# Borders from attention to feed-forward in a new order, two residual adds moved to TensorE, weight pieces stored a tile later

## The chip, the core and the metric

The program runs on one core of one Trainium2 chip. The metric is the device time of one execution in microseconds. TensorE is PE, its weight loads PEld, VectorE DVE, ScalarE ACT, GpSimd POOL; SP (SyncE) issues all DMAs.

## What is computed

Four layers over x of 2048 x 512 (bf16), attention, feed-forward, attention, feed-forward, and then all gradients of that chain for a given grad_out. The two layers, with layernorm LN without scale or shift:

```python
def A(h, wqkv, wo):                       # 32 heads of 16
    q, k, v = split(h @ wqkv)
    pq, pk = phi(q), phi(k)               # phi(t) = where(t > 0, t + 1, exp(t)) + 1e-6
    kv = einsum("bhsd,bhse->bhde", pk, v); z = einsum("bhsd->bhd", pk)
    o = einsum("bhqd,bhde->bhqe", pq, kv) / (einsum("bhqd,bhd->bhq", pq, z)[..., None] + 1e-6)
    return o @ wo
def B(h, w_gate, w_up, w_down):
    return (sigmoid(h @ w_gate) * (h @ w_up)) @ w_down
x = x + A(LN(x)); x = x + B(LN(x)); x = x + A(LN(x)); x = x + B(LN(x))
```

Outputs: the last x and the gradients of x, wqkv, wo, w_gate, w_up and w_down.

## The kernel before

The sequence is cut into 16 tiles of 128 rows (`st`), D = 512 into 4 chunks, F = 1376 into three slices of 512, 512 and 352 columns. Layers 0 and 2 are attention, 1 and 3 feed-forward; the backward part follows. In the forward part PE, ACT, DVE and POOL run in the order in which the code writes their instructions (`manual_schedule`), each engine waiting at the head of its own queue; SP's order is left to the tile scheduler. A DMA issue also waits for the one eight before it.

`kq_fwd` is the attention layer. A loop over tiles makes phi(k) (`pk_all`), phi(q) (`pq_all`, but for the last two tiles) and accumulates X = h^T pk in four PSUM banks. After the loop comes the border: z (sum of pk, broadcast by matmuls with ones), X to SBUF (`X_sb`), kv = Wv^T X masked by head (`kvbdT`), M = kv Wo (`M_sb`), the last two q projections (`late_q`), and MT for the backward part. With M, attention of a tile is one product.

`attn_fronts` has a tile's steps: `prod` (pq times z, POOL or DVE), `front1` (DVE reduces to `den`), `front2` (DVE adds eps, takes the reciprocal `rden_all`, multiplies to `pqnstage`), `front3` (PE transposes it, an engine copies to `pqnT`), `attn_mm` (PE, four matmuls into `y_ps`), `attn_add` (DVE adds the residual into `xs[st]`, then `ln_stats`: bn_stats and bn_aggr on DVE, three small POOL operations). `FwdLN.apply` normalizes on ACT (`hstage`), `stage_T` transposes on PE and copies to `hT`. `attn_y` is `attn_mm` and `attn_add`.

`ab_fwd` is the feed-forward loop. In tile `st` it runs `gu` for three slices (8 matmuls into `g_ps` and `u_ps`, two sigmoids on ACT, `hh_t` on DVE, one multiply into `ssd_t` on POOL), transposes hh into `hhT`, and `finish` of the tile before: 11 matmuls into `y_ps`, the add into `xs` on DVE and, in layer 1 alone, the next layer's `ln_stats`. Between them stand the attention steps of tiles ahead: `FLAG` = 3 for prod and fronts, `YLAG` = 2 for the output. `ssd_t` and `hh_t` have two buffers, so tile st + 2 waits for the stores of tile st. In layer 1 each tile from 1 on also runs one of 13 units of `wT_units`: a transposing load of a weight piece into one of two buffers (`wt_st`), and its store to DRAM for the backward part.

PSUM: `t`, `g`, `u` two banks each, `y` and `ln` one each. All transposes of fronts and `stage_T` share `ln`; attention outputs and `finish` share `y`.

Of the kernel before, what the change touches and what calls it, by code (L numbers as in the profile page):

```python
# [60 lines left out]
def kernel(  # L61
# [78 lines left out]
    with tc.tile_pool(name="wfwd", bufs=1, reuse_waits="tile") as wfwd, ExitStack() as lctx, tc.manual_schedule(engines=EM):  # L140
# [44 lines left out]
        with tc.tile_pool(name="aq0", bufs=1, reuse_waits="tile") as aq:  # L185
            A = kq_fwd(k, aq, 0, lns[0], lns[1], x_bf)
            with tc.tile_pool(name="wt_stage", bufs=2, reuse_waits="tile") as wt_stage:
                units = wT_units(k, wt_stage, A_wqkv, A_wo, B_w_gate, B_w_up, B_w_down)
                A.tail()
                ab_fwd(k, A, lns[1], {st + 1: u for st, u in enumerate(units)}, nxt=lns[2])  # L190
        xctx.close()
        with tc.tile_pool(name="aq2", bufs=1, reuse_waits="tile") as aq:
# [45 lines left out]
            A.tail()  # L238
# [140 lines left out]
def wT_units(k, stage, A_wqkv, A_wo, B_w_gate, B_w_up, B_w_down):  # L379
    nc = k.nc  # L380
    units = []

    def by_rows(src, c0, n, dst):
        def unit():
            t = stage.tile([P, NDC, D], BF16, name="wt_st")
            nfull = min(n, F // P - c0) if src.shape[-1] == F else n
            nc.sync.dma_start(out=t[:, 0:nfull, :], in_=src[:, c0 * P:(c0 + nfull) * P], transpose=True)
            if nfull < n:
                nc.sync.dma_start(out=t[:, nfull, :], in_=src[:, F - P:F], transpose=True)
            nc.sync.dma_start(out=dst[c0 * P:(c0 + nfull) * P, :].rearrange("(n p) d -> p n d", p=P),  # L390
                              in_=t[:, 0:nfull, :])
            if nfull < n:
                nc.sync.dma_start(out=dst[(c0 + nfull) * P:F, :], in_=t[P - FLAST:P, nfull, :])
        return unit

    def by_cols(src, f0, w, dst):
        def unit():
            t = stage.tile([P, NDC, D], BF16, name="wt_st")
            v = t[:].rearrange("p a b -> p (a b)")[:, 0:NDC * w].rearrange("p (a b) -> p a b", a=NDC)
            nc.sync.dma_start(out=v, in_=src[f0:f0 + w, :], transpose=True)  # L400
            nc.sync.dma_start(out=dst.rearrange("(c p) f -> p c f", p=P)[:, :, f0:f0 + w], in_=v)
        return unit

    for f0, w in FSL:
        units.append(by_cols(B_w_down, f0, w, k.wT["wdT"]))
    for src, nm in ((B_w_up, "wuT"), (B_w_gate, "wgT")):
        for c0, n in ((0, 4), (4, 4), (8, 3)):
            units.append(by_rows(src, c0, n, k.wT[nm]))
    for src, nm, C in ((A_wo, "woT", D), (A_wqkv, "wqkvT", 3 * D)):
        for c0 in range(0, C // P, NDC):  # L410
            units.append(by_rows(src, c0, NDC, k.wT[nm]))
    return units
# [20 lines left out]
class FwdLN:  # L433
# [9 lines left out]
    def stats(self, st):  # L443
        if st < NST:
            self.nmr[st] = ln_stats(self.k, self.k.xs[st][:], self.rstd(st))
# [13 lines left out]
    def stage_T(self, st):  # L459
        if st >= NST:  # L460
            return
        k = self.k
        h_t = self.hs.pop(st)
        hT = k.lnres["hT"].tile([P, NDC, P], BF16, name="hT")
        transpose_blocks(k, k.ps["ln"], hT[:], [h_t[:, c * P:(c + 1) * P] for c in range(NDC)], "vector", tag="ln_tp")
        self.hTs[st] = hT
# [60 lines left out]
def kq_fwd(k, aq, l, ln, ln_next, x_src=None):  # L527
# [10 lines left out]
    with ExitStack() as ctx:  # L538
# [4 lines left out]
        if l == 0:  # L543
            MT_sb = big.tile([P, NDC, D], BF16, name="MT_sb")
            X_sb = big.tile([P, NDC, D], BF16, name="X_sb")
        else:
            X_sb = big.tile([P, NDC, D], BF16, name="X_sb")
            MT_sb = big.tile([P, NDC, D], BF16, name="MT_sb")
        cnt = [0]
# [76 lines left out]
        def late_q(st):  # L626
            ps = proj(st, 0, ps_tile(k, "t", [P, D], F32, "t_mm"))
            e_t, a_t = qa_tiles()
            exp_to(e_t, ps)

            def phi():
                clamp(a_t, e_t)
                phi_out(A.pq_all[:, st, :], ps, a_t)
                save_phq(st, a_t)
            return phi
# [69 lines left out]
        z_ps = mm_tile()  # L705
        nc.tensor.matmul(z_ps[:], lhsT=k.ones32[:], rhs=zs, start=True, stop=False)

        def z_mm(st):
            nc.tensor.matmul(z_ps[:], lhsT=k.ones_sq[:], rhs=pk_all[:, st, :], start=False, stop=(st == NST - 1))

        for st in range(NST - ZLAG, NST - 1):
            z_mm(st)
        X_some(NST, NST - 2)
        z_mm(NST - 1)
# [3 lines left out]
        A.front2(0)  # L718
        for ic in range(NDC):
            X_mm(NST - 1, ic)  # L720
            nc.scalar.copy(X_sb[:, ic, :], X_ps[ic][:])
        nc.sync.dma_start(out=sv["X"].rearrange("(c p) j -> p c j", p=P), in_=X_sb[:])

        kv_ps = ps_tile(k, "y", [P, D], F32, "kv_ps")
        kv3 = kv_ps[:].rearrange("p (c f) -> p c f", c=NDC)
        for c in range(NDC):
            cs = slice(c * P, (c + 1) * P)
            for ic in range(NDC):
                nc.tensor.matmul(kv3[:, c, :], lhsT=k.wqkv[:, ic, 2 * D + c * P:2 * D + (c + 1) * P],
                                 rhs=X_sb[:, ic, cs], start=(ic == 0), stop=(ic == NDC - 1))  # L730
        nc.vector.tensor_tensor(kvbdT[:], kv3, k.bdmask[:].unsqueeze(1).to_broadcast([P, NDC, P]), ALU.mult)
        A.front3(0)
        A.prod(1, nc.vector)
        for c in range(NDC):
            m_ps = ps_tile(k, "gu"[c % 2], [P, D], F32, "M_ps")
            nc.tensor.matmul(m_ps[:], lhsT=kvbdT[:, c, :], rhs=k.wo[:, c, :], start=True, stop=True)
            evac_copy(k, A.M_sb[:, c, :], m_ps[:], "vector" if c % 2 else "scalar")
        A.front1(1)
        A.attn_y(0)
        A.front2(1)  # L740
        phis = [late_q(st) for st in range(NST - QLATE, NST)]
        nc.scalar.activation(k.tab[:], k.neg[:], ACT.Sigmoid)
# [6 lines left out]
        A.front3(1)  # L749
        phis[0]()  # L750
        A.ln.apply(0)
        for jc in range(NDC):
            nc.scalar.copy(MT_sb[:, jc, :], mt_ps[jc][:])
        nc.sync.dma_start(out=sv["MT"].rearrange("(c p) j -> p c j", p=P), in_=MT_sb[:])
        A.attn_mm(1)
        phis[1]()
    k.kv[l] = dict(kvbdT=kvbdT, zb=A.zb, rden_all=A.rden_all)

    def tail():
        A.ln.stage_T(0)  # L760
        A.prod(2)
        A.prod(3)
        A.attn_add(1)
        A.front1(2)
        A.front2(2)
    A.tail = tail
# [7 lines left out]
def attn_fronts(k, A, pool, small):  # L774
# [17 lines left out]
    def front2(st):  # L792
# [5 lines left out]
        den = f["den"]  # L798
        f["pqn"] = cur["pqn"][:, st % 2, :]
        nc.vector.tensor_scalar(den[:], den[:], EPS, None, ALU.add)  # L800
        nc.vector.reciprocal(A.rden_all[:, st, :], den[:])
# [6 lines left out]
    def front3(st):  # L808
        if st >= NST:
            return  # L810
        f = F_[st]
        pqnT = pool.tile([P, NDC, P], BF16, name="pqnT", bufs=3)
        transpose_blocks(k, k.ps["ln"], pqnT[:], [f["pqn"][:, c * P:(c + 1) * P] for c in range(NDC)],
                         "scalar", tag="ln_tp")
        f["T"] = pqnT

    def attn_mm(st):
# [3 lines left out]
        y_ps = F_[st]["y"] = ps_tile(k, "y", [P, D], F32, "y_ps")  # L821
        for c in range(NDC):
            nc.tensor.matmul(y_ps[:], lhsT=pqnT[:, c, :], rhs=A.M_sb[:, c, :],  # L823
                             start=(c == 0), stop=(c == NDC - 1))
# [12 lines left out]

    A.attn_mm, A.attn_add = attn_mm, attn_add
    A.prod, A.front1, A.front2, A.front3, A.attn_y = prod, front1, front2, front3, attn_y


def ab_fwd(k, A, ln, side, nxt=None, out_cb=None, last_cb=None):
# [3 lines left out]
    with ExitStack() as ctx:  # L846
# [5 lines left out]
        def gu(T, hT, fs):  # L852
# [4 lines left out]
            for ps, w_sb in ((g_ps, k.wg), (u_ps, k.wu)):  # L857
                for kc in range(NDC):
                    nc.tensor.matmul(ps[:, 0:w], lhsT=hT[:, kc, :], rhs=w_sb[:, kc, c0:c0 + w],  # L859
                                     start=(kc == 0), stop=(kc == NDC - 1))  # L860
            nc.scalar.activation(ssd_t[:, 0, c0:c0 + w], g_ps[:, 0:w], ACT.Sigmoid)  # L861
# [38 lines left out]
        for st in range(NST):  # L900
# [4 lines left out]
                     hhT=wide.tile([P, NFC, P], BF16, name="hhT"))  # L905
            if st == 0:
                gu(T, hT, 0)
                A.front1(FLAG)
                A.front3(2)
                ln.apply(1)  # L910
                gu(T, hT, 1)
                transposes(T, 0)
                A.attn_y(2)
                ln.stage_T(1)
                gu(T, hT, 2)
                A.front2(FLAG)
            else:
                A.prod(st + FLAG)
                gu(T, hT, 0)
                if st == 1:  # L920
                    A.front3(FLAG)
                else:
                    A.attn_y(st + YLAG)
                after(st - 2)
                gu(T, hT, 1)
                if st == 1:
                    A.attn_y(FLAG)
                transposes(T, 0)
                ln.stage_T(st + 1)
                A.front1(st + FLAG)  # L930
                gu(T, hT, 2)
# [4 lines left out]
            ln.apply(st + YLAG)  # L936
# [7 lines left out]
            if st > 0:  # L944
                A.front3(st + FLAG)
            transposes(T, 2)
            nc.sync.dma_start(out=sv["ssd"][rows(st), :, :], in_=T["ssd"][:])
# [765 lines left out]
```

## Time and profile before

| | us |
|---|---|
| median of 3 runs | 1190.37 (1189.86 to 1190.58) |
| profiled execution | 1190.64 |
| its span, first to last instruction | 1188.9 |
| granted TensorE clock | 1.00 throughout |

| engine | busy us (share) |
|---|---|
| PE | 1163.9 (98%) |
| PEld | 705.3 (59%) |
| DVE | 716.9 (60%) |
| ACT | 590.0 (50%) |
| POOL | 290.1 (24%) |

Layer 0's border begins at 54 us of the span, layer 1 runs to 218 us, layer 2's border begins at 259 us and layer 3 ends at 420 us. In a timeline a line holds start, duration, engine, source line, operation, output and inputs, shape and count; a bracket gives the engine's idle time before it and who ended it. PE's busy time includes matmuls that overlap each other's tails.

### The profile page before, as it was taken

How to read it: one execution, taken by the hardware profiler on the slowest of the kernel's cores; microseconds unless marked ns; L12 is line 12 of the kernel's file. 1: busy time of each engine (PE TensorE's matmuls, PEld its weight loads, DVE VectorE, ACT ScalarE, POOL GpSimd, SP SyncE). 2: the span in 40 equal slices, each digit the busy share in tenths (PEclk: the TensorE clock that was granted, in tenths of full speed). 3: DMA queues.
4: the chain of work that ended last, by engine and by line, in shares of the span. 5: the costliest groups of instructions: out<-in, count | busy, mean ns of one | idle time of the engine just before them, and what ended most of it. 6: DMA issues, size and time to landing. Idle time of an engine off the chain costs nothing.

```text
span 1188.9 us, 21404 instructions
## 1 busy us (share of the span) xinstructions
PE 1163.9 (98%) x8106; PEld 705.3 (59%) x8106; DVE 716.9 (60%) x1372; ACT 590.0 (50%) x1092; POOL 290.1 (24%) x496
## 2 busy tenths in 40 slices
PE   8989999998999999999999999999999999999998
PEld 4445455444555555555546568865556745547887
DVE  6788786777777466664975750056664976752111
ACT  6667676546767744443635641154544625630010
POOL 5646665425666400000110010001000110110000
PEclk9999999999999999999999999999999999999999
DMA  8979975458444768977765859468897684749875
GB/s 265 293 194 273 300 251 183 143 170 276 143 170 170 253 189 254 351 206 232 228 196 185 271 156 313 112 178 264 269 285 227 203 280 150 227 116 360 267 202 160
DMA packets 296135, 266.50 MB, mean 224 GB/s; under 512 B 69024, under 2 KB 280928, under 8 KB 291168
## 3 DMA queue, kind: packets, MB, share of 16 engines
q1 hardware_dynamic: 296032, 265.14, 71.4%
q8 instruction: 63, 1.03, 0.4%
q14 instruction: 40, 0.33, 0.1%
HBM read 139.85 MB, written 118.85 MB: 218 GB/s over the span
## 4 chain that ended last, share of the span: by engine, by line
PE 90%; DVE 5%; DMA 2%; ACT 2%; issue 1%; POOL 0%; SPq 0%; DVEq 0%; ACTq 0%; POOLq 0%
PE p_ps L1356 17%; PE dh_ps L1118 13%; PE dh_ps L1571 7%; PE p_ps L1340 6%; PE dhh_ps L1003 6%; PE u_ps L859 5%; PE g_ps L859 5%; PE y_ps L885 5%; PE T_ps L1078 3%; PE GT_ps L1483 2%; PE t_mm L575 2%; PE dpk_ps L1602 2%; PE dp_ps L1458 2%; PE y_ps L823 2%; PE X_ps L583 2%; PE t_tp L873 1%
## 5 line engine op out<-in xcount | busy, mean ns | idle before, releaser
L1356 PE MATMUL p_ps<-p_set,p_a 128*128 128x256 bf16 (+1 forms) x2032 | 210.3, 264 | 0.6 <-DVE dw_stg L1330 0.6
L1356 PEld LDWEIGHTS <-p_a 128*128 128x128 bf16 x2048 | 186.0, 98 | 22.9 <-issue 0.7
L1011 DVE TENSOR_TENSOR dd<-dhh_ps,ssd 128x512 bf16<-128x512 f32 x144 | 82.4, 628 | 134.3 <-PE dhh_ps L1003 129.5
L1082 ACT COPY ddT<-T_ps 128x1024 bf16<-128x1024 bf16 (+1 forms) x96 | 83.0, 867 | 124.7 <-PE T_ps L1078 124.2
L977 POOL TENSOR_SCALAR ab<-c 128x2 f32<-128x2 f32 x64 | 12.3, 193 | 435.6 <-DVE junk L974 422.3
L865 POOL TENSOR_TENSOR ssd_t<-hh_t,oms 128x512 bf16<-128x512 bf16 (+1 forms) x96 | 101.7, 1065 | 50.8 <-ACT out_t L226 38.7
L859 PEld LDWEIGHTS <-hT 128*128 128x128 bf16 x768 | 72.2, 98 | 63.1 <-DVE hT L364 1.4
L1118 PEld LDWEIGHTS <-ddT 128*128 128x128 bf16 (+1 forms) x704 | 67.7, 98 | 69.2
L1330 DVE TENSOR_TENSOR dw_stg<-p_ps,dw_stg 128x512 bf16<-128x512 f32 (+3 forms) x43 | 28.0, 653 | 106.9 <-PE p_ps L1356 78.0
L864 DVE TENSOR_TENSOR hh_t<-u_ps,ssd_t 128x512 bf16<-128x512 f32 (+1 forms) x96 | 60.9, 635 | 52.2 <-PE u_ps L859 35.7
L859 PE MATMUL g_ps<-wg,hT 128*128 128x512 bf16 (+1 forms) x384 | 90.0, 357 | 1.0 <-DVE hT L364 1.0
L859 PE MATMUL u_ps<-wu,hT 128*128 128x512 bf16 (+1 forms) x384 | 90.0, 357 | 0.0
L1118 PE MATMUL dh_ps<-wgT,ddT 128*128 128x512 bf16 (+1 forms) x352 | 86.2, 379 | 0.0
L1003 PE MATMUL dhh_ps<-wdT,gT 128*128 128x512 bf16 x372 | 82.5, 357 | 0.0
L885 PE MATMUL y_ps<-wd,hhT 128*128 128x512 bf16 (+1 forms) x352 | 81.3, 379 | 0.6 <-DVE x L887 0.6
L1118 PE MATMUL dh_ps<-wuT,ddT 128*128 128x512 bf16 (+1 forms) x352 | 81.3, 379 | 0.0
L1340 PE MATMUL p_ps<-p_a,p_set 128*128 128x512 bf16 (+1 forms) x352 | 81.2, 379 | 0.0
L969 ACT ACTIVATE t_sb<-dh_ps,rstd_all 128x512 f32<-128x512 f32 x64 | 44.0, 687 | 72.1 <-issue 38.3
L974 DVE SCALAR_TENSOR_TENSOR junk<-t_sb,h_ld 128x512 bf16<-128x512 f32 x64 | 43.9, 687 | 49.3 <-ACT t_sb L969 48.4
L861 ACT ACTIVATE ssd_t<-g_ps 128x512 bf16<-128x512 f32 (+1 forms) x96 | 53.1, 553 | 26.4 <-PE g_ps L859 23.8
L1332 ACT CAST dw_stg<-p_ps 128x512 bf16<-128x512 f32 (+2 forms) x43 | 24.1, 561 | 65.7 <-PE p_ps L1356 58.8
L876 ACT COPY hhT<-t_tp 128x512 bf16<-128x512 bf16 (+1 forms) x96 | 49.6, 516 | 10.6 <-PE t_tp L873 10.5
(222 smaller groups left out, 2092.1 us busy)
## 6 DMA issues: line engine op xcount, KB each, us to landing
p_set<-sv_hdd SPq DMA_DIRECT2D x30, 1024.0 KB, 6.7
sv_ssd<-ssd_t SPq DMA_DIRECT2D x32, 688.0 KB, 3.9
ssd<-sv_ssd SPq DMA_DIRECT2D x24, 688.0 KB, 5.2
sv_hdd<-dd SPq DMA_DIRECT2D x48, 320.0 KB, 3.7
sv_hdd<-hh_t SPq DMA_DIRECT2D x32, 320.0 KB, 2.6
h_ld<-sv_h SPq DMA_DIRECT2D x32, 256.0 KB, 4.4
p_a<-sv_h SPq DMA_DIRECT2D x16, 512.0 KB, 6.1
p_set<-sv_dqk SPq DMA_DIRECT2D x8, 1024.0 KB, 7.9
```

The costliest lines, as they stand in the source:

```text
L859: nc.tensor.matmul(ps[:, 0:w], lhsT=hT[:, kc, :], rhs=w_sb[:, kc, c0:c0 + w], start=(kc == 0), stop=(kc == NDC - 1))
L861: nc.scalar.activation(ssd_t[:, 0, c0:c0 + w], g_ps[:, 0:w], ACT.Sigmoid)
L864: nc.vector.tensor_tensor(hh_t[:, c0:c0 + w], u_ps[:, 0:w], ssd_t[:, 0, c0:c0 + w], ALU.mult)
L865: nc.gpsimd.tensor_tensor(ssd_t[:, 1, c0:c0 + w], hh_t[:, c0:c0 + w], oms[:, 0:w], ALU.mult)
L885: nc.tensor.matmul(y_ps[:], lhsT=T["hhT"][0:r, fc, :], rhs=k.wd[0:r, fc, :], start=(fc == 0), stop=(fc == NFC - 1))
L1003: k.nc.tensor.matmul(ps[:, 0:w], lhsT=gT[:, jc, :], rhs=k.wdT[:, jc, c0:c0 + w], start=(jc == 0), stop=(jc == NDC - 1))
L1011: k.nc.vector.tensor_tensor(dd[:, a, c0:c0 + w], ps[:, 0:w], ssd[:, a, c0:c0 + w], ALU.mult)
L1082: nc.scalar.copy(ddT[:, :, f0:f0 + nfull, :], tps[:, :, 0:nfull, :])
L1118: nc.tensor.matmul(T["dh"][:], lhsT=ddT_block(T, a, fc), rhs=(k.wuT, k.wgT)[a][0:r, fc, :], start=(i == 0), stop=(i == 2 * NFC - 1))
L1340: nc.tensor.matmul(ps[0:r, :], lhsT=set_t[:, st, c * P:c * P + r], rhs=self.ops[j["l"], "g"][:, st, :], start=(st == 0), stop=(st == NST - 1))
L1356: nc.tensor.matmul(ps[:, icl * w:(icl + 1) * w], lhsT=self.ops[j["l"], "h"][:, st, ic * P:(ic + 1) * P], rhs=set_t[:, st, 0:w], start=(st ...
L1571: nc.tensor.matmul(dh_ps[:], lhsT=lhsT, rhs=rhs, start=(i == 0), stop=(i == len(ops) - 1))
```

## The change

In the border, `z_ps` moves from the rotating banks to `y`, `kv_ps` from `y` to `ln`; z's matmuls no longer alternate with X's; the kv matmuls run chunk by chunk of X_sb, each followed by four of the first late q projection; M is made in one go; the reciprocal of tile 0 is taken early (`rden`). Outputs of tiles 0 and 1 no longer use `attn_add`: `attn_res` puts the residual into `y_ps` by a matmul with an identity (bf16 in layer 0, f32 `eye32` in layer 2), `attn_mm` adds onto it, and `attn_out` takes the statistics from PSUM and copies to `xs` on ACT. `keep_on` puts unused matmuls into the border (2 + 3 + 2 in layer 0, 3 in layer 2). `tail` is gone: prod(2) stands before tile 1's fronts, prod(3) at the head of tile 0. In `ab_fwd` the attention outputs of tiles 2, 3 and 4 move to tiles 1, 2 and 2, with their statistics, applies and transposes. Each weight piece is stored at the tile after its load.

```diff
@@ wT_units
-            nc.sync.dma_start(out=dst[...], in_=t[:, 0:nfull, :])      (and the remainder, by_rows and by_cols alike)
+            def store():
+                nc.sync.dma_start(out=dst[...], in_=t[:, 0:nfull, :])
...
+            stores.append(store)
-    return units
+    def step():
+        old = stores[:]
+        stores.clear()
+        if units:
+            units.pop(0)()
+        for store in old:
+            store()
+    return [step] * (len(units) + 1)
@@ kq_fwd
+        def keep_on(n):
+            ps = ps_tile(k, "ln", [P, D], F32, "on_ps")
+            for _ in range(n):
+                nc.tensor.matmul(ps[:], lhsT=k.ident[:], rhs=pk_all[:, 0, :], start=True, stop=True)
...
         A.prod(0, nc.vector)
         A.front1(0)
-        A.front2(0)
+        X_some(NST, NST - 2)
         for ic in range(NDC):
             X_mm(NST - 1, ic)
-            nc.scalar.copy(X_sb[:, ic, :], X_ps[ic][:])
+            evac_copy(k, X_sb[:, ic, :], X_ps[ic][:], "vector" if ic == NDC - 1 else "scalar")
+        A.rden(0)
...
+        for ic in range(NDC):
+            for c in range(NDC):
+                nc.tensor.matmul(kv3[:, c, :], lhsT=k.wqkv[:, ic, ...], rhs=X_sb[:, ic, cs], ...)
+            nc.tensor.matmul(q_ps[:], lhsT=hTs[NST - 2][:, ic, :], rhs=k.wqkv[:, ic, 0:D], ...)
         nc.vector.tensor_tensor(kvbdT[:], kv3, k.bdmask[:]..., ALU.mult)
+        phis = [late_q(NST - 2, q_ps)]
+        A.front2(0, False)
+        A.attn_res(0, eye)
+        if l == 0:
+            keep_on(2)
         (M: 4 matmuls, copies on ACT, ACT, DVE, DVE)
         A.front3(0)
+        phis.append(late_q(NST - 1))
+        nc.scalar.activation(k.tab[:], k.neg[:], ACT.Sigmoid)
+        phis[0]()
+        A.attn_mm(0)
+        A.attn_out(0)
         A.prod(1, nc.vector)
+        A.prod(2)
         A.front1(1)
         A.front2(1)
         (MT: 16 matmuls)
+        mt_copy(0)
+        mt_copy(1)
         A.ln.apply(0)
+        keep_on(3)
+        A.attn_res(1, eye)
+        if l == 0:
+            keep_on(2)
+        A.front3(1, "vector")
+        mt_copy(2)
+        A.ln.stage_T(0, "scalar")
+        phis[1]()
+        A.attn_mm(1)
+        mt_copy(3)
+        A.attn_out(1)
-    def tail():
-        A.ln.stage_T(0)
-        A.prod(2)
-        A.prod(3)
-        A.attn_add(1)
-        A.front1(2)
-        A.front2(2)
@@ attn_fronts
+    def attn_res(st, ident):
+        y_ps = F_[st]["y"] = ps_tile(k, "y", [P, D], F32, "y_ps")
+        nc.tensor.matmul(y_ps[:], lhsT=ident[:], rhs=..., start=True, stop=False)   (the residual)
+    def attn_out(st):
+        y_ps = F_.pop(st)["y"]
+        A.ln.stats(st, y_ps[:])
+        nc.scalar.copy(k.xs[st][:], y_ps[:])
@@ ab_fwd, tiles 0 to 2 after
+            A.prod(st + FLAG)
+            st 0: front1(2) rden(2) gu0 front2(2) apply(1) gu1[stage_T(1) between its matmuls and its sigmoids]
+                  transposes0 gu2 front3(2) transposes1 transposes2
+            st 1: gu0 attn_y(2) front1(3) gu1 front2(3) transposes0 gu2 apply(2) front1(4) front3(3)
+                  transposes1 finish(0) stage_T(2) front2(4) transposes2
+            st 2: gu0 attn_y(3) front3(4) apply of layer 2's LN(0) gu1 attn_y(4) transposes0 front1(5) gu2
+                  apply(3) front2(5) transposes1 stage_T(3) finish(1) front3(5) transposes2 apply(4)
```

(The last six lines name the steps of the new code in their order.) From tile 3 on the order is the old one.

## The prediction

> **What bounds the kernel now.** I read the page's chain first, then windows by border and tile, then the engines' timelines in the border. TensorE carries the end, so a microsecond counts only where PE's queue loses or gains it:
>
> ```profile
> PE 90%; DVE 5%; DMA 2%; ACT 2%; issue 1%; POOL 0%; SPq 0%; DVEq 0%; ACTq 0%; POOLq 0%
> ```
>
> The first two windows run from the z matmul (L706) to tile 1's first y_ps matmul (L885), for each layer pair; the others are tiles of layer 1 (window, us, PE, PEld, DVE, ACT, POOL busy, clock, DMA share, GB/s):
>
> ```profile
> 53.97:94.39 40.42, 33.99 (x226) 17.92 (x225) 31.48 (x63) 26.96 (x52) 19.04 (x30) 1.00 0.76 222
> 258.86:299.21 40.35, 33.99 (x226) 17.93 (x225) 30.18 (x60) 26.64 (x52) 18.69 (x27) 1.00 0.77 253
> 112.62:121.57 8.95, 8.95 (x62) 4.81 (x60) 7.63 (x15) 6.71 (x14) 5.94 (x10) 1.00 1.02 281
> 121.57:130.83 9.26, 9.12 (x61) 4.80 (x59) 7.90 (x15) 6.70 (x14) 6.57 (x12) 1.00 1.19 284
> 130.83:140.87 10.04, 9.30 (x62) 4.64 (x60) 6.83 (x15) 6.48 (x14) 5.80 (x9) 1.00 1.05 355
> 140.87:150.43 9.56, 9.12 (x61) 4.79 (x59) 8.19 (x16) 6.51 (x13) 6.81 (x13) 1.00 1.08 285
> ```
>
> Busy PE holds matmul tails; what PE must issue is less. From starts in PE's timeline a 512-wide matmul takes 0.216 us (g_ps 72.87, u_ps 73.73, four between), a 352-wide 0.149, a 128-wide 0.0555, the f32 512-wide 0.86 (53.97 to 54.83). A border window needs 101, 24, 98 and 1 of these: 21.8 + 3.6 + 5.4 + 0.9 = 31.7 us. So each border loses 40.4 - 31.7 = 8.7 us. The marks (idle before, releaser) say where:
>
> ```profile
> 57.45 0.22 PE L729 MATMUL kv_ps<-X_sb,wqkv 128*128 128x128 bf16 x1 [0.30 <-ACT X_sb L721]
> 67.35 1.04 PE L823 MATMUL y_ps<-M_sb,pqnT 128*128 128x512 bf16 x4 [1.00 <-ACT pqnT L366]
> 72.64 0.40 PE L357 MATMUL ln_tp<-ident,pqnstage 128*128 128x128 bf16 x4 [1.60 <-DVE pqnstage L802]
> 78.32 0.34 PE L873 MATMUL t_tp<-ident,hh_t 128*128 128x128 bf16 x3 [0.83 <-DVE hh_t L864]
> ```
>
> (marks count from the matmul's end, so each is 0.1 to 0.2 short of what PE's queue loses): X_sb copies 1.8, M 0.75, M_sb 0.45, pqnT(1) 0.5 + 1.1, hT(0) 0.7, pqn(2) 1.7, hh 1.0, pqn(4) 0.5. Layer 1 loses 1.09 + 0.29 = 1.4 more in two tiles (10.04 and 9.56 against 8.95 and 9.27): ACT waits for an old ssd store, as the waits say (us in total, times, longest):
>
> ```profile
> ACT ssd_t L861 <- DMA sv_ssd<-ssd_t: 2.0, 1, 2.0
> ```
>
> **Added PE work.** The residual as a matmul: two bf16 of 0.216 at the first border; at the second x is f32, so two of 0.86 (z's row is the only f32 512-wide one). keep_on: 7 matmuls at the first border (1.51), 3 at the second (0.65). The clock reads 1.00 in every window, so they buy no clock; they cost unless they stand in a gap, which the gap count below decides. Sum +1.94 and +2.37.
>
> **Where PE will wait.** I laid the new order of every queue out with the durations of before. In place of the 8.7 I get:
> - X_sb: four q matmuls (4 x 0.216) between the kv steps leave 0.3 of 1.8.
> - z's last matmul, without X matmuls in front, waits 0.4 for pk at the first border only; the first keep_on (a PSUM buffer that kv_ps holds) 0.5, likewise; M_sb/pqnT(0) and attn_res 0.3; hh(0) 0.4 instead of 1.0.
> - pqn(1): behind attn_mm(0) PE has MT, keep_on and attn_res, 2.2 to 2.4 us. DVE's chain is 0.20 to start, bn_stats 0.72 (now from PSUM; every 512-wide f32 row, PSUM or SBUF, is 0.69), aggr 0.1, prod 0.45, reduce 0.71, add 0.21, reciprocal 0.38, pqnstage. With pqnstage at 1.43 (below) and 0.05 to wake PE the chain is 4.25, the gap 1.9 and 1.7 (attn_res's own wait of 0.15 is part of what PE does).
> - hT(0): ps_ln has one buffer, so h(0)'s transposes wait until DVE has copied pqnT(1): 0.2 tail, copy 0.42, two wake-ups, 0.65.
> - pqn(3): from the second slice's last u_ps DVE is 0.6 in its reduce, then hh 0.60, add 0.20, reciprocal 0.39, pqnstage 1.31, 0.1 to wake PE: 3.2. PE has four transposes and the third slice, 0.22 + 1.19: gap 1.8.
> - hT(2): its transposes now stand behind finish(0), its DVE copy behind finish's x add and, in layer 1 alone, bn_stats and aggr. After the last y_ps issue: 0.20 + 0.72 + 0.72 + 0.10 + 0.42 + 0.05 = 2.2, less 7 transposes (0.39): 1.85; without statistics 0.9.
> - hT(3): transposes ahead of finish(1), apply(3) on ACT behind two 352-wide sigmoids: 0.2 + 0.36 + 0.36 + 0.81 + 0.05 = 1.78 after g_ps, less u_ps and four transposes (0.82): 1.0.
>
> Together 9.0 at the first border, 7.0 at the second. Against 8.65 from the same layout of the old order (measured 8.7): +0.4 and -1.6.
>
> **The price of pqnstage.** In SBUF-only DVE work beside POOL work, the later starter ends late (start, duration, engine, line):
>
> ```profile
> 58.73 0.69 DVE L802 TENSOR_TENSOR pqnstage<-pq_all,rden_all 128x512 bf16<-128x512 bf16 x1
> 86.35 0.85 POOL L865 TENSOR_TENSOR ssd_t<-hh_t,oms 128x352 bf16<-128x352 bf16 x1
> 86.71 1.04 DVE L802 TENSOR_TENSOR pqnstage<-pq_all,rden_all 128x512 bf16<-128x512 bf16 x1
> 78.77 0.69 DVE L802 TENSOR_TENSOR pqnstage<-pq_all,rden_all 128x512 bf16<-128x512 bf16 x1
> 78.82 1.35 POOL L865 TENSOR_TENSOR ssd_t<-hh_t,oms 128x352 bf16<-128x352 bf16 x1
> ```
>
> At 86.71 DVE ends 0.55 after POOL's end; at 78.77 DVE came first and POOL paid (0.85 became 1.35). In the old border pqn(1) and pqn(2) met no POOL work. In the new one prod(2) (1.15) starts 0.26 before pqn(1) (the old row: prod 1.58 after aggr; DVE's prod, reduce, add and reciprocal take 1.84), and the multiply of slice 2 0.4 before pqn(3). So 1.43 and 1.31 instead of 0.69: 0.74 + 0.62 = 1.36 per border, 2.7 in all, inside the gaps above. Bounds: 0 if DVE wins each, 2.7 if POOL does; I take POOL, since both leads are over a quarter microsecond. The Trainium skill, "SBUF — State Buffer", section "Who interferes with whom", says that such a pair is an exclusive lock and the second fully blocks. By a full block each pqnstage would end 0.69, not 0.55, after POOL: 0.6 more in all. The trace agrees on who pays and differs by that 0.14.
>
> **Weight pieces, and DMAs that move.** A piece's store goes out one tile later, behind the next piece's load. In SP's new order a store still waits for its load at the head of the queue, with ssd, hdd and sv_h stores behind it. With successive landings of before (ssd 1.7, hdd 0.95, transposed load 2 to 3.5, weight store 1.25) tile 5's ssd store lands 2 us before tile 7's sigmoid needs it (in the old order it is just late); the closest is hdd(5), 0.4 ahead of DVE's first hh(7). So the 1.4 goes: -1.4; bounds -1.4 and 0. The sv_pqn, sv_phq and X stores move by one or two places; their buffers are written again two tiles later or never, and no PE wait of before names them: 0, and a late sv_pqn would cost what pqnstage then waits.
>
> The rest is 0: two x adds leave DVE (0.69 each) and x copies enter ACT (0.59), neither last in any gap above; prod(2) and prod(3) move on POOL, costed with pqnstage; eye32 is built before its border; outputs of tiles 3 and 4 do the same work in other places and by tile 2 the order is the old one.
>
> **Sum.** +1.94 + 0.4 + 2.37 - 1.6 - 1.4 = +1.7. The profiled execution was 1190.64 (span 1188.9, 1.74 around it), so 1192.3; the median of the runs is 0.27 lower, so 1192.1. Behind the borders all shifts as a block: the backward part is PE's own queue.
>
> A measurement of this kernel can tell about 0.2%, 2.4 us, from no change: below 1188.0 is faster, above 1192.75 slower.
>
> **Rivals.**
> - *SP's queue, slower.* The store waits at the head of SP's queue until its transposed load has landed (4 to 7 us after issue in the DMA view), and the ssd store of a tile stands behind it. For: issues already take 1 to 2 us there, DMA share is over 1.0. Against: 2 us of slack by my landings. From 2 us more delay on, the 1.4 stays, and a second tile may lose 1.1: +3.1 to +4.2, 1193.5 to 1194.6.
> - *POOL is not in the way.* If DVE comes first at pqn(1) and pqn(3), 2.7 goes: 1189.4. For: 0.26 is a small lead. Against: in the second border POOL's prod starts 1.59 after aggr (269.36 to 270.95), as in the first.
> - *The borders fill.* If hT(2) and hT(3) too are covered (their evacuations in time), 1.85 + 0.9 + 2.0 more goes: 1184.7. Against: the DVE order behind finish is fixed.
>
> **Chances.** Forecast 0.57 (of it 0.40 within 0.2%, 0.17 above, for its unknowns of about 1 us); SP's queue 0.22 (0.20 slower); POOL 0.15 (0.12 within, 0.03 faster); filled borders 0.06. Faster 0.09, same 0.54, slower 0.37. The range takes in the forecast, POOL out of the way and most of SP's queue: 1189.4 to 1194.6.
>
> **What would show it.** Right: borders of about 42.8 and 41.1 us in the same windows; PE idle before ln_tp released by pqnstage at 1.3 to 1.4 us, before tile 2's g_ps released by hT, longer in layer 1 than in 3; no ACT wait for sv_ssd. Wrong: pqnstage at 0.69 in the border, ACT or DVE waiting for a store, or a border under 40.

## The result and the profile after

Changed kernel: 1193.60 us median of 9 executions (1192.16 to 1196.67); kernel before beside it: 1190.39 (1189.86 to 1191.62). Ratio 1.0028, 95% interval 1.0019 to 1.0037: slower by 0.28%, a little more than the 0.2% that can be told. A second set gave 1.0032 (1.0021 to 1.0044). The median lies inside the predicted range and 1.5 us above the predicted time, and the spread grew: 4.5 us against 1.8.

The profiled execution took 1192.16 us (span 1190.4), the lowest of its set: remember this when its lines agree with the prediction. Its chain:

```profile
PE 91%; DVE 5%; DMA 1%; ACT 1%; issue 1%; SPq 0%; DVEq 0%; POOL 0%; POOLq 0%
```

PE carries the end as before. The windows: the two borders and then four tiles of layer 1, the last two those in which the old kernel lost time (window, us, PE, PEld, DVE, ACT, POOL busy, clock, DMA share, GB/s):

```profile
53.67:96.55 42.88, 35.53 (x236) 18.56 (x235) 32.24 (x63) 27.78 (x54) 19.84 (x29) 1.00 0.76 221
259.60:300.68 41.08, 35.73 (x234) 18.70 (x233) 30.95 (x60) 27.63 (x54) 18.48 (x26) 1.00 0.73 236
114.75:123.70 8.95, 8.95 (x62) 4.79 (x59) 7.63 (x15) 6.70 (x14) 5.94 (x10) 1.00 1.00 293
123.70:132.97 9.27, 9.13 (x62) 4.81 (x60) 7.91 (x15) 6.71 (x14) 6.58 (x12) 1.00 1.07 238
132.97:141.91 8.94, 8.94 (x61) 4.78 (x59) 7.10 (x15) 6.70 (x14) 5.90 (x10) 1.00 0.94 290
141.91:151.20 9.29, 9.13 (x63) 4.81 (x60) 7.94 (x15) 6.71 (x14) 6.62 (x12) 1.00 1.07 324
```

The borders are 42.88 and 41.08 (before 40.42 and 40.35, predicted 42.8 and 41.1). The tiles of 10.04 and 9.56 are 8.94 and 9.29: in this execution no tile is longer for a store, and what is left of ACT's wait of 2.0 is this:

```profile
ACT ssd_t L911 <- DMA sv_ssd<-ssd_t: 0.3, 1, 0.3
```

The gaps in the borders, from PE's timeline (start, duration, instruction, idle before and releaser):

```profile
67.61 0.40 PE L355 MATMUL ln_tp<-ident,pqnstage 128*128 128x128 bf16 x4 [1.62 <-DVE pqnstage L836]
68.53 0.38 PE L355 MATMUL ln_tp<-ident,hstage 128*128 128x128 bf16 x4 [0.52 <-DVE pqnT L362]
75.56 0.34 PE L923 MATMUL t_tp<-ident,hh_t 128*128 128x128 bf16 x3 [0.24 <-DVE hh_t L914]
83.27 0.40 PE L355 MATMUL ln_tp<-ident,pqnstage 128*128 128x128 bf16 x4 [1.64 <-DVE pqnstage L836]
88.31 1.04 PE L907 MATMUL g_ps<-wg,hT 128*128 128x512 bf16 x4 [1.65 <-DVE hT L362]
96.31 0.40 PE L355 MATMUL ln_tp<-ident,hstage 128*128 128x128 bf16 x4 [0.79 <-ACT hstage L440]
...
292.44 1.04 PE L907 MATMUL g_ps<-wg,hT 128*128 128x512 bf16 x4 [0.72 <-DVE hT L362]
```

These are pqn(1), hT(0), hh(0), pqn(3), hT(2), hT(3), and hT(2) of layer 3: with 0.1 to 0.2 added for the tail they are, within 0.1, the 1.9, 0.65, 0.4, 1.8, 1.85, 1.0 and 0.9 of the prediction. The price of pqnstage beside POOL, from the timelines of DVE and POOL:

```profile
65.86 1.15 POOL L814 TENSOR_TENSOR prod<-pq_all,zb 128x512 bf16<-128x512 bf16 x1
66.16 1.40 DVE L836 TENSOR_TENSOR pqnstage<-pq_all,rden_all 128x512 bf16<-128x512 bf16 x1
81.52 1.15 POOL L915 TENSOR_TENSOR ssd_t<-hh_t,oms 128x512 bf16<-128x512 bf16 x1
81.84 1.37 DVE L836 TENSOR_TENSOR pqnstage<-pq_all,rden_all 128x512 bf16<-128x512 bf16 x1
```

POOL starts 0.30 and 0.32 ahead, and DVE ends 0.55 and 0.54 after POOL: 1.40 and 1.37, forecast 1.43 and 1.31.

So the profile follows the sum (borders +2.46 and +0.73, tiles -1.4, and a first border that begins 0.3 earlier by chance, at 53.67 instead of 53.97), and the median does not: this execution is 1.5 above the old profiled one, the median 3.2 above the old median. The runs weigh four theories. **Sum theory**: only the terms of the prediction's sum count, the same in every execution. **Work theory**: every matmul costs what it issues. **Clock theory**: the granted clock falls in some executions because PE idles too much in a border. **Queue theory**: a store lands late in some executions.

### The profile page after: what moved, and what is told of

Same layout as the page of the kernel before. It is cut to its first block, busy times and chain, and to the rows that moved or that the text cites. A ratio compares the mean times of both kernels' runs of the same rounds, so it can differ in the third digit from the quotient of the medians.

```text
span 1190.4 us, 21442 instructions
## 1 busy us (share of the span) xinstructions
PE 1166.9 (98%) x8122; PEld 707.0 (59%) x8122; DVE 718.4 (60%) x1370; ACT 590.3 (50%) x1094; POOL 289.5 (24%) x498
## 4 chain that ended last, share of the span: by engine, by line
PE 91%; DVE 5%; DMA 1%; ACT 1%; issue 1%; SPq 0%; DVEq 0%; POOL 0%; POOLq 0%
PE p_ps L1424 17%; PE dh_ps L1186 13%; PE dh_ps L1639 7%; PE p_ps L1408 6%; PE dhh_ps L1071 6%; PE g_ps L907 5%; PE y_ps L935 5%; PE u_ps L907 5%; PE T_ps L1146 3%; PE GT_ps L1551 2%; PE dp_ps L1526 2%; PE dpk_ps L1670 2%; PE y_ps L870 2%; PE t_mm L592 2%; PE X_ps L600 2%; PE t_tp L923 1%
```

## The experiments

The granted clock of an execution is its mean to three places; a border's drop, one elsewhere and the moments after the last matmul all enter it, so it counts drops without placing them. Borders are those of the one profile. "Below" counts executions with a mean under 1.000; for the kernel before, run beside these, it was 18 of 73. Its medians in the sets were 1190.87 to 1191.47.

| kernel | median (range), n | ratio, 95% interval | below | borders |
|---|---|---|---|---|
| again | 1194.72 (1192.25-1197.51), 8 | 1.0032, 1.0021-1.0044 | 5 of 8 | 44.20, 41.08 |
| no_keep | 1195.84 (1193.80-1198.51), 6 | 1.0039, 1.0026-1.0051 | 6 of 6 | 45.23, 41.09 |
| old_store | 1195.05 (1193.99-1197.16), 5 | 1.0034, 1.0022-1.0046 | 4 of 5 | 42.36, 42.56 |
| late_store | 1192.40 (1191.03-1193.59), 11 | 1.0011, 1.0002-1.0019 | 1 of 11 | 40.44, 40.36 |
| sp_b | 1199.01 (1198.34-1199.47), 5 | 1.0071, 1.0057-1.0084 | 5 of 5 | 40.43, 40.36 |
| sp_b_late | 1189.91 (1189.01-1191.58), 11 | 0.9989, 0.9981-0.9998 | 4 of 11 | 40.44, 40.36 |
| sp_a | 1195.97 (1192.96-1197.09), 5 | 1.0040, 1.0027-1.0053 | 4 of 5 | 42.87, 41.08 |
| sp_fill | 1194.38 (1193.03-1196.13), 6 | 1.0029, 1.0018-1.0041 | 1 of 6 | 42.37, 41.19 |
| sp_prod | 1192.80 (1191.69-1194.78), 11 | 1.0018, 1.0009-1.0027 | 3 of 11 | 42.22, 40.58 |
| sp_ht2 | 1194.37 (1191.27-1195.91), 12 | 1.0021, 1.0012-1.0031 | 9 of 12 | 42.62, 40.85 |
| sp_res | 1197.85 (1196.29-1198.94), 5 | 1.0052, 1.0038-1.0066 | 5 of 5 | 44.29, 43.36 |
| best | 1189.71 (1187.84-1192.84), 11 | 0.9992, 0.9983-1.0000 | 3 of 11 | 38.59, 39.76 |

In four profiles (old_store, sp_fill, sp_ht2, best) the gap before z's last matmul (0.34 by its mark) is missing, and border 1 is 0.5 shorter for that alone.

**The changed kernel again** (no edit).

> The changed kernel once more, for a second profile and more times. Sum theory (only the terms of the prediction's sum, the same in every execution): every execution has borders of 42.9 and 41.1 us, time 1192.2 to 1192.8, spread under 2 us as with the kernel before. Clock theory (the gaps of 1.3 to 2 us in the new border let the granted clock fall for a while in some executions): median 1193.6, a spread of 4 to 5 us, and in a slow profile a stretch near a border with a granted clock of 0.5 and matmuls at twice their interval. Queue theory (a store lands late in some executions): the same spread, but at a granted clock of 1.00, with ACT or DVE waiting for sv_ssd or sv_hdd in layer 1.

Its profile caught a drop. Four windows of 3.41 us (the eighth column is the granted clock):

```profile
61.35:64.77 3.42, 3.42 (x32) 2.01 (x30) 2.95 (x6) 3.23 (x5) 0.00 (x0) 1.00 0.13 41
64.77:68.18 3.41, 1.61 (x10) 0.57 (x9) 3.04 (x6) 2.90 (x7) 2.24 (x4) 1.00 0.01 2
68.18:71.59 3.41, 2.90 (x14) 1.36 (x12) 1.58 (x4) 1.07 (x2) 0.00 (x0) 0.50 0.32 115
71.59:75.01 3.42, 3.42 (x20) 1.64 (x19) 3.25 (x7) 2.91 (x6) 2.42 (x5) 1.00 1.05 271
```

In the second, PE is busy 1.61 us: it holds most of the gap before pqnstage(1). In the next the clock is 0.50 and 14 matmuls pass. The border takes 44.20 instead of 42.88: one drop costs 1.3 us. Layer 1 loses another 0.25 to stores (a tile of 9.52). Both clock and queue theory hold something.

**Without keep_on.**

```
-        if l == 0:
-            keep_on(2)          (after attn_res(0))
-        keep_on(3)              (before attn_res(1))
-        if l == 0:
-            keep_on(2)          (after attn_res(1))
```

> The changed kernel without its keep_on matmuls (7 in the first border, 3 in the second, results unused). Sum theory: they stand in gaps that the DVE chain behind attn_mm(0) and the kvbdT multiply set anyway, so 0 to -0.4 us against the changed kernel, same spread. Work theory (they cost what they issue): -1.5 and -0.65, 2.2 us faster. Clock theory: the gaps get longer without them, 2 to 3 us each, so the granted clock falls in more executions: median 1 to 4 us slower than the changed kernel and a wider spread. Queue theory: spread as with the changed kernel.

```profile
63.95:67.36 3.41, 0.99 (x12) 0.49 (x9) 3.17 (x7) 3.40 (x7) 2.24 (x4) 1.00 0.08 26
67.36:70.77 3.41, 2.44 (x12) 1.42 (x13) 1.72 (x4) 1.21 (x3) 0.00 (x0) 0.50 0.32 115
70.77:74.19 3.42, 3.42 (x10) 1.18 (x8) 1.99 (x5) 1.80 (x4) 1.66 (x4) 0.50 0.73 191
```

PE is busy 0.99 us of the starved window, the clock stays at 0.50 for two windows, the border is 45.23, and not one of six executions keeps 1.000, against 10 of 17 with the matmuls. The work theory (2.2 us faster) is out: the ten matmuls that nobody reads cost nothing that shows. The median is 1.1 to 1.9 above the changed kernel's, 1194.72 beside it and 1193.95 for its 17 executions together. That is clock theory's size, but the intervals of no_keep and again overlap and the spread (4.7) is not wider, so the counts and the profile bear the theory out, not the median.

**Stores at once, in the new border; stores late, in the old border.** The old wT_units in the changed kernel (old_store), and the new wT_units in the kernel before (late_store).

> The changed kernel with each weight piece stored at once, as before (the borders stay new). Sum theory: the ACT wait for sv_ssd comes back in layer 1, two tiles of 10.0 and 9.5 instead of 8.95 and 9.25, so +1.4 us against the changed kernel. Queue theory (late stores cause the spread): the spread goes back to under 2 us, and the median falls to 1193 or below in spite of the 1.4. Clock theory: spread stays at 4 to 5 us, median +1.4.

> The kernel before with the weight pieces stored a tile later, nothing else. Sum theory: -1.4 us, 1189.0, spread under 2 us, no ACT wait for sv_ssd. Queue theory: the late stores bring the spread, median 1190 to 1193 and single executions 3 to 5 us above the fastest. Clock theory: as sum theory.

Late stores alone make the kernel before 1.5 us slower (by the interval 0.2 to 2.3), where the prediction had them 1.4 faster. The waits of late_store in layer 1 (us in total, times, longest; before: 2.0, 1, 2.0), and its tiles where before has 10.04, 9.56 and 8.95:

```profile
DVE hh_t L876 <- DMA sv_hdl<-hh_t: 4.9, 3, 2.8
ACT ssd_t L873 <- DMA sv_ssd<-ssd_t: 3.0, 3, 2.1
...
130.74:140.83 10.09, 9.30 (x62) 4.64 (x59) 6.82 (x15) 6.48 (x14) 5.78 (x9) 1.00 0.92 289
140.83:150.94 10.11, 9.36 (x62) 4.63 (x59) 7.37 (x16) 6.59 (x13) 6.28 (x11) 1.00 1.05 300
150.94:160.50 9.56, 9.12 (x62) 4.80 (x59) 7.96 (x16) 6.45 (x13) 6.74 (x13) 1.00 0.85 240
```

The wait did not go; it grew and found a third tile and another store (sv_hdl). In the new border old_store lost 0.6 + 0.7 + 0.3 in three tiles (9.87, 9.67, 9.57), about the 1.4 of sum theory, and its second border caught a drop (42.56 instead of 41.08). Its median is only 0.3 above that of again, where 1.4 was expected, and its spread (3.2) fits neither theory's number. But late stores in the new border are no cure either: 0 lost in the first profile, 0.25 in again, 1.5 + 0.3 in no_keep. What the pieces cost seems to depend on where SP's queue stands when the tiles need it, in each order anew; the next runs set that order.

**SP's order as the code writes it.** The scheduler issues all 13 pieces between 70 and 157 us, that is by tile 8; the edit gives each its own tile:

```
+                with tc.manual_schedule(engines=EM | {mybir.EngineType.SP}):
                     ab_fwd(k, A, lns[1], {st + 1: u for st, u in enumerate(units)}, nxt=lns[2])
```

sp_b has it on the kernel before, sp_b_late on late_store, sp_a on the changed kernel. All runs behind these (sp_fill, sp_prod, sp_ht2, sp_res, best) start from sp_a.

> The kernel before with SP's order in layer 1 as the code writes it (one weight piece per tile, tiles 1 to 13) in place of the scheduler's (all pieces by 157 us, that is by tile 8). Nothing else changes. Queue theory (layer 1 loses 1.4 to 2.3 us because the pieces crowd into tiles 2 to 8 and the queue falls behind): no ACT or DVE wait for a store, all tiles 8.95 and 9.27, -1.4 us or a little more: 1189.4 or less. Rival (the queue was not the reason, the store's own latency is): tiles 5 and 6 stay at 10.0 and 9.5, time as before.

> The kernel before with weight pieces stored a tile later and SP's order as the code writes it: the two edits that by themselves cost 1.5 and 8 us. Queue theory: in the changed kernel the same pair left layer 1 without a wait, so here too: no wait for a store, all tiles 8.95 and 9.27, 1.4 us under the kernel before: 1189.5. It is then the clean base for the borders: the changed kernel with the same SP order has borders 2.45 and 0.7 longer. Rival (the waits in tiles 10 to 14 come from the code order itself): +5 to +8 us as without the late stores.

> The changed kernel with SP's order in layer 1 as the code writes it. It takes the store waits out of the comparison: what is left between this and the same edit of the kernel before is the borders and the clock. Sum theory: +1.94 + 0.4 + 2.37 - 1.6 = +3.1 us against that kernel, spread under 2 us. Clock theory: the median stands 1 us or more above its own fastest execution and the spread stays at 3 to 5 us, with the granted clock below 1.000 in the slow ones.

In sp_b tiles 2 to 9 are clean (8.95, 9.27), as queue theory has it, and then it loses 8 us from tile 10 on, where the old order lost nothing. There PE issues nothing for a whole clock window and the clock falls; all five executions have a mean under 1.000. In the code's order a piece's store stands right behind its own transposed load and holds SP's queue until that has landed, with the next tile's stores behind it. The waits for a store in layer 1, and one of SP's own, of a weight store (L391) for its load:

```profile
ACT ssd_t L862 <- DMA sv_ssd<-ssd_t: 7.2, 2, 3.9
DVE hh_t L865 <- DMA sv_hdl<-hh_t: 9.8, 3, 4.7
SPq L391 <- DMA wt_st<-in_A_wqkv_dram: 5.9, 2, 3.5
```

With the store a tile later there is nothing to wait for: in sp_b_late SP waits for no weight load, and there is no wait for a store on ACT or DVE in layer 1, all its tiles are 8.95 and 9.25, and it is 1.27 us under the kernel before, the predicted 1.4. Each of the two edits alone is slower; together they are faster. That is why the profiles of sp_a and sp_b_late, both clean, compare the borders alone (sp_a was to be held against sp_b, 3.1 above it; sp_b was not clean): spans of 1191.21 and 1187.48, 3.7 us apart, of it 2.43 + 0.72 in the borders and 0.6 because sp_b_late's first border begins earlier. The medians stand 6.1 apart: four of sp_a's five executions lie under 1.000, and the one at 1.000 took 1192.96.

**Filling the gap.** 7 (second border 4) more keep_on:

```
-        keep_on(3)
+        keep_on(10 if l == 0 else 7)
         A.attn_res(1, eye)
```

> The same with 7 more keep_on matmuls (4 in the second border) in front of attn_res(1), that is inside the gap of 1.9 and 1.7 us in which PE waits for pqnstage(1): 1.5 and 0.9 us of matmuls whose results nobody uses. Sum theory: they fit into the gap, so the same time and the same spread as without them. Clock theory: the window that starves is this one, so the drops go: median 1 to 1.5 us lower than without, granted clock 1.000 in every execution, spread under 2.5 us. Work theory (any added matmul costs its issue): +2.4 us.

```profile
68.33 0.40 PE L356 MATMUL ln_tp<-ident,pqnstage 128*128 128x128 bf16 x4 [0.45 <-DVE pqnstage L837]
```

Work theory (2.4 slower) is out again. The gap before pqnstage(1)'s transposes shrinks to 0.45 (from 1.62) and the borders do not grow (by 0.1 in the second; the first lacks z's 0.5); five of six executions keep 1.000, against one of five in sp_a. The median falls by 1.6, as clock theory has it, though the intervals of the two runs overlap and the spread is 3.1 and not under 2.5.

**prod(2) on DVE.**

```
-        A.prod(2)
         A.front1(1)
         A.front2(1)
+        A.prod(2, nc.vector)
```

> The same (without the extra keep_on) with prod(2) on DVE behind pqnstage(1) instead of on POOL beside it. Sum theory: pqnstage(1) takes 0.69 instead of 1.43, so each border is 0.7 shorter: 42.2 and 40.4, -1.4 us. Rival (POOL is not what makes it slow): pqnstage(1) stays at 1.4, time the same or 0.1 longer for the later pqnT copy. Clock theory adds to the sum: a gap 0.7 shorter lets the clock fall in fewer executions, so the median falls by 2 or more.

```profile
66.87 0.69 DVE L837 TENSOR_TENSOR pqnstage<-pq_all,rden_all 128x512 bf16<-128x512 bf16 x1
```

0.69 instead of 1.40, with nothing changed but POOL's work beside it, and borders 0.65 and 0.50 shorter: POOL is what makes it slow, and the term of 0.74 is the right size (the rival is out). The median falls by 3.2, more than the 1.15 of the borders; 8 of 11 executions keep 1.000. Clock theory forecast such an extra; with five executions of sp_a its size is uncertain.

**hT(2) evacuated by ACT.**

```
-                ln.stage_T(2)
+                ln.stage_T(2, "scalar")
```

> The changed kernel with SP's order as the code writes it, and stage_T(2)'s evacuation on ACT instead of DVE. Sum theory: the DVE chain behind finish(0) (x add, in layer 1 also bn_stats and aggr) no longer stands before g_ps(2). ACT's own copy behind the transposes leaves a gap of about 0.7: 1.85 becomes 0.7 in the first border, 0.9 becomes 0.7 in the second, so borders of 41.7 and 40.9, -1.3 us in all. Rival (ACT is as late as DVE, behind its sigmoids): the gap stays at 1.5 or more. Clock theory: the window that starves is that of pqnstage(1), 20 us earlier, so the share of executions with a granted clock under 1.000 stays as high as without.

```profile
89.57 1.04 PE L908 MATMUL g_ps<-wg,hT 128*128 128x512 bf16 x4 [0.51 <-ACT hT L365]
```

The mark falls from 1.65 to 0.51, in the second border from 0.72 to 0.51 (40.85 instead of 41.08): -1.14 and -0.2, as forecast. Its profile has a drop in the first border, so that 42.62 hides the gain there. And 9 of 12 executions stay under 1.000: shortening a gap elsewhere saves its own length and does nothing for the window of pqnstage(1). The same clock behaviour as sp_a, although 1.1 us of idle PE went, is what tells the two gaps apart.

**The residual back on DVE.**

```
-        A.attn_res(0, eye)
-        A.attn_res(1, eye)
-        A.attn_out(0)
+        A.attn_add(0)
-        A.attn_out(1)
+        A.attn_add(1)
```

> The changed kernel with SP's order as the code writes it, and the residual of tiles 0 and 1 added by DVE again (x add of 0.7 before bn_stats) instead of by attn_res on PE and a copy on ACT. Work theory (a matmul costs its issue): 2 x 0.216 and 2 x 0.86 us less, -2.15 us. Sum theory: DVE's chain from attn_mm(0) to pqnstage(1) grows by the add, from 4.25 to 4.97, and PE has 0.2 (0.86) less to do in that gap, and the same add stands before tile 1's statistics: the gaps grow by more than the work that goes, borders 1.3 longer each, 44.2 and 42.3, +2.6 us. Clock theory adds: the gap before pqnstage(1)'s transposes is then 2.8 us, so the granted clock falls in nearly every execution.

```profile
275.23 0.40 PE L356 MATMUL ln_tp<-ident,pqnstage 128*128 128x128 bf16 x4 [3.26 <-DVE pqnstage L835]
```

PE has 2.15 us less to do and the borders are longer: 44.29 (+1.42), and 43.36 with a drop in it (granted clock 0.96 over the border), where 42.3 was expected without one. The gap before pqnstage(1) is 2.7 and 3.26 by the marks, and all five executions lie under 1.000. So the residual on PE gains 1.4 us in the first border, and about 0.8 to 1.0 in the second, if the drop costs 1.5 as in old_store's second border or 1.3 as in again, although it costs two f32 matmuls there: what it takes off is DVE's chain, which ends last.

**Everything together.** best is sp_prod and sp_ht2 together with two more moves, fewer keep_on before M and more in the gap:

```
+                A.front2(3)             (st 1: before gu1 instead of behind it)
+            if st == 2:
+                ln.apply(3)             (before gu2 instead of behind it)
-        if l == 0:
-            keep_on(2)                  (after attn_res(0))
-        keep_on(3)
+        keep_on(7 if l == 0 else 6)
```

> The changed kernel with SP's order as the code writes it, prod(2) on DVE behind pqnstage(1), pqnstage(3) before the second slice's hh instead of behind it, stage_T(2) evacuated by ACT, apply(3) ahead of the third slice's sigmoids, the two keep_on before M left out and seven (six) instead of three before attn_res(1). Sum theory: against 42.9 and 41.1 the terms are -0.7 -0.7 (pqnstage(1) and (3) without POOL beside them; the third also without hh ahead, -0.4) -1.15 (-0.2) for hT(2), -0.7 for hT(3) in both, -0.4 for keep_on: borders, counted over the two following tiles too, 3.5 and 2.5 us shorter, and no wait for a store: 1187 to 1188, below both kernels. Clock theory: gaps all under 0.8 us, so granted clock 1.000 in every execution and a spread of 2 us or less. Rival (the clock falls for the sum of gaps, not for one): spread of 3 to 5 us remains, median 1189 to 1190.

Borders (the next tile is 0.5 longer than 8.95, so 0.5 comes back):

```profile
55.33:93.92 38.59, 35.79 (x237) 18.66 (x236) 29.70 (x60) 27.55 (x54) 17.63 (x27) 1.00 0.45 144
257.44:297.20 39.76, 36.25 (x236) 19.06 (x235) 28.83 (x58) 27.31 (x54) 16.65 (x24) 1.00 0.77 244
```

The first fell as expected (4.07 with the two tiles behind it, 0.5 of it z's gap). The second fell by 0.8 over the same stretch where 2.5 was expected: PE waits 1.44 for hh there instead of 0.24, behind an ACT copy that starts 1.3 late; the trace does not say why, and that stays open. Of 11 executions 8 keep 1.000 and the spread is 5.0: clock theory's forecast (all at 1.000, 2 us or less) failed, and the rival's numbers came, a spread of 3 to 5 and a median of 1189 to 1190. Its reason, that gaps under 0.8 add up, was not tested further. It is 1.5 us under the kernel before, with an interval that just reaches no change, and 0.4% under the changed kernel (0.9992 against 1.0028 and 1.0032). sp_b_late does as well with the old borders, 0.9989, so the medians show nothing of what best's borders save: its profile begins the first border 1.7 later (55.33 against 53.63) and waits 1.6 longer near 1158 us (see the last section).

## Why the prediction came out as it did

**Borders: right.** Forecast +1.94 + 0.4 and +2.37 - 1.6, measured +2.46 and +0.73. The gaps stand where they were laid and within 0.2 of their size. X_sb's 0.3 leaves no mark, but the starts show it: X's eight matmuls are issued by 57.20 and kv begins at 57.38, and two later kv steps begin 0.05 late. pqnstage beside POOL was forecast at 1.43 and 1.31 and took 1.40 and 1.37, and sp_prod shows for the first of the two that the cause was the right one. The Trainium skill ("SBUF — State Buffer", "Who interferes with whom") has the second of the pair wait until the first is done: DVE would then end 0.69 after POOL; it ended 0.55 and 0.54 after.

**Weight stores: wrong.** "So the 1.4 goes: -1.4" rests on landings laid one behind the other with 2 us to spare. The first profile bears it out, the runs do not: late_store is 1.5 slower than before, and in the new border the loss was 0, 0.25 and 1.8 in three profiles. The step that failed is the slack: 2 us for ssd(5), and "the closest is hdd(5), 0.4 ahead of DVE's first hh(7)". With the queue full in these tiles (DMA share about 1.0) neither margin held from one order and one execution to the next: in late_store ssd_t waited up to 2.1 and hh_t up to 2.8 (for sv_hdl), in again up to 0.7 and 1.6. The rival of SP's queue named this mechanism; it came true in part. What removes the waits is the pair of one piece per tile and the store a tile later (sp_b_late).

**The clock: not seen.** "The clock reads 1.00 in every window, so they buy no clock" was true of the one execution shown and wrong as a step. keep_on does buy clock: 0 of 6 executions at 1.000 without it (no_keep), 10 of 17 with it, 5 of 6 with more of it (sp_fill, against 1 of 5 in sp_a). The gap of pqnstage(1), which the sum prices at 1.9 (1.8 by the starts), costs 1.3 more in the executions in which one window falls on it and the wait around it.

**How the miss of 1.5 divides.** The changed kernel's executions at 1.000 have a median of 1193.5 (10 of 17), those below 1196.1; for the kernel before it is 1190.8 (55 of 73) and 1192.4. At 1.000 the change costs 2.7, against 1.7 of the sum. The 1.0 between would fit a store term of 0.4 instead of 1.4 on the average, but no run shows that it is all stores: the start of the first border and the wait near 1158 us (last section) move single executions by as much. The rest, some 0.4 of the median, goes with the clock. Of the 2.6 between executions below and at 1.000 one drop in the border explains 1.3; the other half is open. This division is worked out from medians, not shown by one run. That the median lies inside the range is in part luck: the range reaches up to 1194.6 for the rival of SP's queue, and the clock has no term in it.

**A basis that did not hold.** The sum was moved from the profiled execution to the median by -0.27, the old kernel's difference. The changed kernel's profiled execution was its lowest, 1.4 below its median.

## What to carry to other kernels

Price a gap on TensorE twice: by its length, and by whether it and its neighbours can leave one clock window starved; matmuls that nobody reads, put inside such a gap, cost nothing here and held the clock more often, and taking away the POOL work beside a DVE multiply shortens gap and risk at once. Do not book a saving for a transfer that is to land a fraction of a microsecond earlier in a queue that is full: change how much is in the queue, or what it waits for, and look at several executions. A profile is one execution: compare its time with the others' before its lines are taken for the kernel's.

## What the hardware showed that was not expected

- **A clock window can starve without an idle window.** Drops last 3.41 us or twice that. Summing PE's issue times over windows of 3.41 us in the phase of each profile's drops and clock edges (thirteen profiles; sp_a's has no record of the clock), the window ahead of each of six drops had PE issuing 0.00 to 0.38 of the time; of the others the lowest were 0.36 (once) and 0.38. So the edge lies near there and is not sharp. In again no single idle stretch before the drop was longer than 1.62 us. The Trainium skill ("TensorE: Matmul & The Clock Gate", "Part 1: The HAM clock gate (the "warmup" mystery)") says that the window is free-running and about 3.4 us long, and that the clock falls after an idle window. Length and free phase agree with these traces; the condition does not: half busy by the profile's row (1.61 of 3.41) was too little. To come back took more: after a window at 0.50 with PE busy 2.90 of it (again) the clock was full, after one with 2.44 (no_keep) it was not.
- **Which executions drop.** The phase of the windows differs from run to run, so the same kernel drops in some executions and not in others: 7 of 17 were under 1.000 with the scheduler's SP order, 13 of 17 with the code's (sp_a and sp_ht2 together, whose borders have the same gap before pqnstage(1)). The counts are too small to say that the order matters.
- **Two more sources of spread, outside the change.** The first border begins at 53.63 to 55.33 us in the fourteen profiles, and at 53.67 to 55.33 in the ten whose code up to there is the same; no run tells why. And near 1158 us, in the backward part, PE waits for dw_stg, which waits for an output store. In most profiles, the two kernels' own among them, PE's wait is 0.5 to 0.7; in sp_prod, sp_fill, sp_ht2, old_store and best it is 1.9 to 2.2, and the span is 1.3 to 1.6 longer for it. From sp_prod's waits:

```profile
DVE dw_stg L1399 <- DMA out_dram<-dw_stg: 4.8, 1, 4.8
PE p_ps L1425 <- DVE dw_stg L1399: 2.0, 1, 2.0
```

No run here tells what decides it.
